# The first expert slot's up products and half of its down products move into attention's instruction list

## The chip, the cores and the metric

The kernel runs on one core of a Trainium2 chip. The metric is the device time of one execution in microseconds (us), compared as the median of several executions. A run's profile is one more execution with the hardware profiler on. PE is the matrix engine, DVE the vector engine, ACT the scalar engine, POOL the general engine, SP the engine whose queue issues most DMAs.

## The reference

Three stages follow each other, all in float32: attention through a packed set of 32 keys, a mixture of 8 experts with one expert per token, and a gated dense layer.

```python
# attention: B=8, H=8, S=576, D=64, 32 packed queries p
p_packed = sm_attn(p, k, v)                 # softmax(p k^T / 8) v
out      = sm_attn(q, p_packed, p_packed)   # softmax(q pp^T / 8) pp
x = out.transpose(0, 2, 1, 3).reshape(4608, 512)
# experts: expert_idx = argmax of cosine(x, expert_emb) / tau
for e in range(8):
    h = np.maximum(x[mask] @ w1[e], 0.0)        # 512 -> 1024
    out[mask] = gate_w[mask, None] * (h @ w2[e])  # 1024 -> 512
# dense: 512 -> 1536 -> 512
return ((x @ w_a) * (x @ w_b)) @ w_out
```

## The kernel before

Attention works through eight batches. For one batch it transposes k (L302), multiplies it with the packed queries (L332, L336), takes the softmax, transposes it (L381) and multiplies it with v (L397): that gives `pp`, the packed values. Then q is transposed (L490), multiplied with `pp` (L528, in two units of 4 and 5 blocks), put through a second softmax on DVE and ACT (L535 to L553), transposed (L560, copied to `aT`), and multiplied with the Gram matrix of `pp` (L581), which gives norms and dot products for the routing (`sq` L590, `nd`).

The experts work in 16 slots of 288 tokens, two for a batch. The kernel takes all tokens of a batch to belong to one expert and falls back to a general path if they don't. Since x = A pp, the first layer is A (pp w1): `zed` computes z = pp w1 (L1008, two products of 16 matmuls a batch), split into a high and a low part (`zh` on ACT, `zl` on DVE). Every expert product is three matmuls of split parts (`mm3`, L816 to L818). A slot has four up products of 24 small steps in two halves, 12 matmuls each, followed by relu (`hh` on ACT, L1069, and `hl` on DVE, L1073), and four down products of 24 matmuls each, followed by a copy to `y` (L1097). w2 is split by `split_w` into `w2h` (ACT, L1039) and `w2l` (DVE, L1040).

Nothing reorders at run time: every engine works through its list in order. The lists are written by a planner (`Sched`), which takes the operations with their engine, cost, priority and buffers, and places at each step the ready operation of the lowest priority number. `SHIFT` adds a number to the priority of each kind of operation; `VB` is a handicap of DVE against ACT for copies that either can do (`evict`). There are two lists: attention's, and then one for the expert slots. `before` puts the first loads, the z products of batch 0 and the splits of its A into attention's list; the slots themselves are in the second list (`static`).

On-chip memory in attention: PSUM holds four one-bank tiles `tr` (transposes, small products) and two two-bank tiles `two` (scores, `pp`, L581, z). The second list has its own PSUM tiles in the same banks, three `up` and two `dn`. Keys and values lie in three tiles each on the right side of SBUF. The w1 loads of a batch and the w2 loads of batch 0 use the same four tiles `raw`, so w2 of batch 0 can be loaded only when both z products of batch 0 are done.

The routing of batches 4 to 7 is the first thing that the second list has in PSUM tile `up` (L743, L744); it goes on to DVE (L747, L748), to POOL for a square root as a power (L751), and back to DVE (L721).

```python
e_ops, g_ops = experts(nc, c, pool(st, "b_rt", side="right", reuse_waits="tile"), KNOWN, B, up0)
e = chain(sch, e_ops, 0.0, c.late, "up", 0.01)
```

Of the kernel before, what the change touches and what calls it, by code (L numbers as in the profile page):

```python
# [7 lines left out]
F32 = mybir.dt.float32  # L8
# [67 lines left out]
class Sched:  # L76
# [96 lines left out]
    "aT_ev.f": -18.7, "aT_mm.f": 98.4, "chain.<lambda>": 59.55, "eT_ev.<lambda>": -79.65,  # L173
    "eT_mm.f": -26.2, "fetch.ar": -2.25, "fetch.pr": -86.75, "kT_ev.<lambda>": 90.1, "kT_mm.f": -142.9,
    "load_k.<lambda>": 20.4, "load_v.<lambda>": 25.1, "make_consts.ev": -33.8, "make_consts.mm": -185.0,
    "ppT_ev.f": 74.65, "pp_mm.f": -143.1, "prep.exp": -130.55, "prep.gr_ev": 11.4, "prep.gr_mm": -194.4,
    "prep.keep": 52.0, "prep.load_p": -79.5, "prep.m8_ev": 0.85, "prep.mx": -10.8, "prep.pT_ev": -78.4,
    "prep.pT_mm": 27.65, "prep.ppT_mm": 43.1, "prep.ppx_a": -211.2, "prep.ppx_ev": -78.55,
    "prep.rs": -114.6, "prep.s1_mm": 226.05, "query.<lambda>": 18.2, "query.qT_ev": 72.75,
    "query.qT_mm": 158.95, "rest.add": 273.9, "rest.dots": -206.3, "rest.exp": 42.6, "rest.mx": 52.8,  # L180
    "rest.norm": -54.4, "rest.s2_mm": -70.25, "rest.sq": 67.35, "rest.sub": 90.45, "rest.total": 172.2,
    "rest.x_mm": -100.75, "split_a.<lambda>": 62.0, "split_w.<lambda>": -222.8, "w1.f": -76.15,
    "w2.f": 35.55, "zed.<lambda>": -92.6, "zed.mm": -87.75}


def attention(ctx, tc, c, q, k, v, p, a_dram, pT_dram, consts, more):
# [28 lines left out]
    S_.LAT, S_.VB, S_.SHIFT, S_.LF = 0.22, 0.25, SHIFT, 4.3  # L215
# [29 lines left out]
    ppT_ops, gr_ops, c.kept, c.a_kept = {}, {}, {}, {}  # L245
# [6 lines left out]
    def prep(b):  # L252
# [58 lines left out]
        for m in (0, 1, 2, 3, 4):  # L311
            t = Buf("tr")
            bkT.append(Buf(f"kT{m}" if m < 4 else "kt"))
            o = op({"T": 0.44}, kT_mm(m), mm=4, deps=[o_k[m // 2]] if m < 4 else o_k, prio=at(0.05 * m), take=[t, bkT[m]],
# [90 lines left out]
        for i0, i1 in ((0, 4), (4, 8), (8, 9)):  # L405
# [4 lines left out]
            mms.append(op({"T": 0.2 * (i1 - i0)}, pp_mm(i0, i1), mm=8 * (i1 - i0), deps=[o] + o_v + mms[-1:], prio=at(0.6 + 0.01 * i0),  # L410
                          take=[] if i0 else [bs], free=[beT] + bv))

        for g in range(2):
# [53 lines left out]
            o = op({"T": 0.42}, gr_mm, mm=10, deps=ppT_ops[b, g], prio=f(0.9), take=[t], free=[bT])  # L467
# [6 lines left out]
    def query(b):  # L474
# [10 lines left out]
        for x in range(5):  # L485
# [14 lines left out]
            o = op({"T": 0.44}, qT_mm, mm=4, deps=o_q + o_qT[-2:-1], prio=pr, take=[tr, bqT[x]], free=bq)  # L500
# [401 lines left out]
class Moe:  # L902


    class Ring:

        def __init__(self, pool, n, shape, dt, name):
            self.t = [pool.tile(shape, dt, tag=f"{name}{i}", name=f"{name}{i}") for i in range(n)]
            self.i = 0
# [8 lines left out]
    def __init__(self, tc, c, pool, raws, a_dram, pT_dram, x2T, w1, w2):  # L918
# [5 lines left out]
        self.ar = [pool.tile([128, 2, S], F32, name=f"ar{i}") for i in range(2)]  # L924
# [5 lines left out]
        self.bufs, self.o_zmm = {}, {}  # L930

    def open(self, pool, up, dn):
        R = self.Ring
        self.r_hh, self.r_hl = R(pool, 4, [128, 2, SLOT], F32R, "hh"), R(pool, 4, [128, 2, SLOT], F32R, "hl")
        self.raw2 = self.raw2[:4] + [pool.tile([128, 1024], F32, name=f"rawb{i}") for i in range(4)]
        self.wt += [[pool.tile([128, 8, 128], F32R, name=f"w2{x}{i}") for x in "hl"] for i in (2, 3)]
        self.r_y = R(pool, 2, [128, 2, SLOT], F32, "y")
        self.r_up = R(up, 3, [128, 2, 512], F32, "up")
        self.r_dn = R(dn, 2, [128, 512], F32, "dn")


    def fetch(self, S, b, p, speak, a_kept, kept):
# [21 lines left out]
        for k in range(4):  # L964
            o = ld[b, "ra", k] = op({"D": 1.46}, w1(k), deps=[speak, first], prio=p + 0.1 * k, take=[Bf(f"ra{k}")],
                                    lat=2.0)
            first = first or o
        ld[b, "pr"] = op({"D": 0.8}, pr, deps=kept, prio=p, take=[Bf("pr")], lat=2.0)
        ld[b, "ar"] = op({"D": 1.6}, ar, deps=[a_kept], prio=p + 0.3, take=[Bf("ar")], lat=2.0)
# [4 lines left out]
    def fetch2(self, S, b, p):  # L974
# [11 lines left out]
        for i in range(4):  # L986
            self.bufs[b, f"rb{i}"] = Buf(f"{n}{i}")
            self.o_ld[b, "rb", i] = op({"D": 1.6}, w2(i), deps=[self.o_ld[b, "ra", 0]], prio=p + 0.1 * i,
                                       take=[self.bufs[b, f"rb{i}"]], lat=2.0)
# [53 lines left out]
    def before(self, S, psum, prio, speak):  # L1043
# [6 lines left out]
        self.zed(S, 0, prio + 1.0, "two", psum)  # L1050
# [3 lines left out]
        for i in range(2):  # L1054
            self.split_w(S, 0, i, prio + 3.0)


# [45 lines left out]
    def static(self, S, speak, flag):  # L1103
# [4 lines left out]
        y_ops = {}  # L1108
# [18 lines left out]
        for s in range(2):  # L1127
            held(None, self.bufs[s, "at"])

# [13 lines left out]
        for s in range(NS):  # L1143
            b, half = divmod(s, 2)
            ups, hls, bh = [], [], []
            for i in range(4):
                bu, st, h = Buf("up"), {}, Buf("h")
                bh.append(h)
                p = s + 0.08 * i

                def mm(e, i=i, st=st, s=s):
                    st["ps"] = self.up_mm(s, i)

                o = op({"T": 1.62}, mm, deps=[self.o_z[b, g, i // 2] for g in range(2)] + [self.o_a[s]], prio=p,
                       take=[bu], free=[self.bufs[s, "at"]] + [self.bufs[b, "z", g, i // 2] for g in range(2)])
                ups.append(o)
# [755 lines left out]
```

## Time and profile before

| what | value |
|---|---|
| median of 3 runs | 1348.51 us (1348.19 to 1353.03) |
| profiled execution, its own time | 1352.98 us |
| its span, first to last instruction | 1350.8 us |
| PE busy / weight loads | 1314.0 us (97%) / 1209.8 us (90%) |
| DVE, ACT, POOL busy | 780.9 (58%), 585.6 (43%), 99.5 us (7%) |
| mean granted clock of PE | 0.993 of full speed |

Busy time of PE counts a matmul from its start to its modelled end, so a busy PE can still be paced by something else; its idle time is certain. The granted clock has two levels here, full (2.4 GHz, shown as 1.0) and half (1.2 GHz); a mean between them says what part of a stretch ran at half.

### The profile page before, as it was taken

Reading aid. Unit: us, or ns where it says so; the run is one execution under the profiler, and the core shown is the slowest. Engines: PE = TensorE matmul, PEld = TensorE weight load, DVE = VectorE, ACT = ScalarE, POOL = GpSimd, SP = SyncE. Lnnn points to the kernel's source line nnn. Section 1 sums busy time; section 2 is a strip of 40 time slices with the busy share of each in tenths; the row PEclk is TensorE's granted clock in tenths of the full one; section 3 lists DMA queues with packets and bytes.
Section 4 is the critical chain, followed back from the end, with each engine's and each line's share of the span. In section 5 each row is a group of like instructions: output and inputs, shape, how many; then the busy total and the mean of one; then the engine's idle time right before and its main releaser. Section 6 shows DMA issues by size and latency. Waiting matters only on the chain.

```text
span 1350.8 us, 25483 instructions
## 1 busy us (share of the span) xinstructions
PE 1314.0 (97%) x9731; PEld 1209.8 (90%) x9731; DVE 780.9 (58%) x1503; ACT 585.6 (43%) x1238; POOL 99.5 (7%) x223
## 2 busy tenths in 40 slices
PE   7999889999999999999999999999999999999997
PEld 6887679999999998999899989999999989999996
DVE  4777866767666828888543454435543563434342
ACT  5765534544444526565432343325332443343232
POOL 1012020010010100000200020002000100001002
PEclk9999989999999999999999999999999999999999
DMA  8875498777797527776855585557656766556552
GB/s 282 285 228 184 155 298 268 249 244 265 227 292 237 181 90 264 240 269 238 251 160 160 158 249 159 160 158 241 170 156 164 228 178 157 162 169 191 162 157 65
DMA packets 169265, 275.34 MB, mean 204 GB/s; under 512 B 18984, under 2 KB 68520, under 8 KB 169136
## 3 DMA queue, kind: packets, MB, share of 16 engines
q1 hardware_dynamic: 162704, 254.72, 61.8%
q0 software_dynamic: 6272, 18.88, 4.0%
q8 instruction: 80, 1.31, 0.4%
q14 instruction: 49, 0.40, 0.1%
q10 hardware_dynamic: 160, 0.02, 0.0%
HBM read 217.99 MB, written 55.57 MB: 203 GB/s over the span
## 4 chain that ended last, share of the span: by engine, by line
PE 91%; DVE 3%; DMA 3%; ACT 1%; issue 1%; POOL 0%; SPq 0%; ACTq 0%; DVEq 0%
PE o L1736 7%; PE o L1737 7%; PE o L1738 7%; PE pb L816 6%; PE pb L818 6%; PE pb L817 6%; PE pa L816 6%; PE pa L818 6%; PE pa L817 6%; PE dn L816 5%; PE dn L818 5%; PE dn L817 5%; PE up L816 3%; PE up L817 2%; PE up L818 2%; DMA out_dram<-osb 2%
## 5 line engine op out<-in xcount | busy, mean ns | idle before, releaser
L1487 DVE TENSOR_TENSOR s<-s,s 128x384 f32<-128x384 f32 x324 | 176.7, 556 | 342.1 <-ACT s L1623 339.6
L816 PE MATMUL pb<-xq,wq 128*128 128x384 f32 x504 | 170.8, 339 | 2.7 <-ACT s L1623 1.1
L816 PE MATMUL pa<-xq,wq 128*128 128x384 f32 x504 | 170.2, 338 | 1.6 <-DVE s L1487 1.6
L1736 PE MATMUL o<-oh,gh 128*128 128x512 f32 x432 | 170.5, 395 | 0.9 <-ACT osb L1756 0.9
L1738 PE MATMUL o<-oh,gl 128*128 128x512 f32 x432 | 170.4, 395 | 0.0
L818 PE MATMUL pa<-xq,wq 128*128 128x384 f32 x504 | 170.3, 338 | 0.0
L1737 PE MATMUL o<-ol,gh 128*128 128x512 f32 x432 | 170.2, 394 | 0.0
L818 PE MATMUL pb<-xq,wq 128*128 128x384 f32 x504 | 170.0, 337 | 0.0
L817 PE MATMUL pb<-xq,wq 128*128 128x384 f32 x504 | 169.8, 337 | 0.0
L817 PE MATMUL pa<-xq,wq 128*128 128x384 f32 x504 | 169.7, 337 | 0.0
L816 PE MATMUL dn<-hh,w2h 128*128 128x288 f32 x512 | 152.6, 298 | 0.0
L1623 ACT COPY s<-pa 128x384 f32<-128x384 f32 x180 | 86.4, 480 | 149.2 <-PE pa L818 149.0
L817 PE MATMUL dn<-hl,w2h 128*128 128x288 f32 x512 | 151.0, 295 | 0.0
L818 PE MATMUL dn<-hh,w2l 128*128 128x288 f32 x512 | 150.6, 294 | 0.0
L1623 ACT COPY s<-pb 128x384 f32<-128x384 f32 x180 | 86.4, 480 | 142.4 <-PE pb L818 142.3
L816 PEld LDWEIGHTS pb<-xq,wq 128*128 128x128 f32 x504 | 94.6, 188 | 13.5 <-DVE c L1487 2.1
L816 PEld LDWEIGHTS dn<-hh,w2h 128*128 128x128 f32 x512 | 95.9, 187 | 9.2 <-ACT hh L1069 3.4
L816 PEld LDWEIGHTS pa<-xq,wq 128*128 128x128 f32 x504 | 94.6, 188 | 9.9 <-DVE s L1487 2.2
L817 PEld LDWEIGHTS pb<-xq,wq 128*128 128x128 f32 x504 | 94.7, 188 | 8.5
L817 PEld LDWEIGHTS pa<-xq,wq 128*128 128x128 f32 x504 | 94.7, 188 | 7.5
L1738 PEld LDWEIGHTS o<-oh,gl 128*128 128x128 f32 x432 | 81.0, 187 | 19.1
L818 PEld LDWEIGHTS dn<-hh,w2l 128*128 128x128 f32 x512 | 96.4, 188 | 0.0
(199 smaller groups left out, 2367.7 us busy)
## 6 DMA issues: line engine op xcount, KB each, us to landing
wq<-ws SPq DMA_DIRECT2D x420, 256.0 KB, 2.8
ws<-wq SPq DMA_DIRECT2D x84, 256.0 KB, 3.8
raw<-in_moe_w_dram SPq DMA_DIRECT2D x36, 512.0 KB, 6.3
rawb<-in_moe_w_dram SPq DMA_DIRECT2D x28, 512.0 KB, 8.2
k<-in_k_dram SPq DMA_DIRECT2D x16, 576.0 KB, 5.1
v<-in_v_dram SPq DMA_DIRECT2D x16, 576.0 KB, 6.3
q<-in_q_dram SPq DMA_DIRECT2D x16, 576.0 KB, 6.3
xr<-x2T SPq DMA_DIRECT2D x20, 384.0 KB, 4.3
```

What stands on the lines that cost most here:

```text
L816: nc.tensor.matmul(ps, lhsT=wh, rhs=xh, start=start, stop=False, **kw)
L817: nc.tensor.matmul(ps, lhsT=wh, rhs=xl, start=False, stop=False, **kw)
L818: nc.tensor.matmul(ps, lhsT=wl, rhs=xh, start=False, stop=stop, **kw)
L1487: VT = lambda out, a, b, o: V.tensor_tensor(out=out, in0=a, in1=b, op=o)
L1623: A.copy(out=T[n, key], in_=ps[n, names_bank[key]])
L1736: nc.tensor.matmul(a, lhsT=gh[:, h, s], rhs=wh, start=first, stop=False)
L1737: nc.tensor.matmul(a, lhsT=gh[:, h, s], rhs=wl, start=False, stop=False)
L1738: nc.tensor.matmul(a, lhsT=gl[:, h, s], rhs=wh, start=False, stop=last)
```

## The change

The four up products and the first two down products of slot 0 are taken out of the second list and put into attention's (`ups` and `downs`, called from `before`). There they use attention's PSUM tiles: up products the two `two` tiles, down products the `tr` tiles. The tiles for relu's results (`hh`, `hl`) and for `y` are opened in the middle of attention's list: the pool that holds keys and values moves to the left side of SBUF, is closed by `swap`, and the new pool takes its place once the last transposes of k and the last products with v are placed. One of the two tiles for A, `ar1`, moves from a pool that lives from the start to one that is opened with the second list. The number of matmuls, their shapes and what they compute stay as they are.

With it go new planner numbers: all of `SHIFT`, `VB` from 0.25 to 0.45, a cost of four kinds of PE work, and a delay of 4.0 instead of 2.0 for the first expert's loads. So attention's whole order is another one. For instance the first loads were p, k, k, v and are now k, k, k, p. Over the whole program 16 small copies go from DVE to ACT (40 such copies were on DVE, 24 are).

```diff
-    "aT_ev.f": -18.7, "aT_mm.f": 98.4, "chain.<lambda>": 59.55, "eT_ev.<lambda>": -79.65,
+    "aT_ev.f": 118.2, "aT_mm.f": -41.15, "before.<lambda>": -65.3, "chain.<lambda>": 161.7,
...
-    for name, pools in dict(io="kvq", kt=["pT", "pz", "kt"] + [f"kT{m}" for m in range(4)], q=["qT"], e=["e", "eT"],
+    for name, pools in dict(io="q", kt=["pT", "pz", "kt"] + [f"kT{m}" for m in range(4)], q=["qT"], e=["e", "eT"],
...
+    sb.update(k=c.kv, v=c.kv)
...
-    S_.LAT, S_.VB, S_.SHIFT, S_.LF = 0.22, 0.25, SHIFT, 4.3
+    S_.LAT, S_.VB, S_.SHIFT, S_.LF = 0.22, 0.45, SHIFT, 4.3
...
         for i in range(2):
             self.split_w(S, 0, i, prio + 3.0)
-
+        self.r_up, self.r_dn = two, one
+        room = S.op({"none": 0.0}, lambda e: self.open_h(c.swap()), deps=c.over(), prio=prio)
+        self.hls, self.bh = self.ups(S, 0, prio + 4.0, "two", [room])
+        self.downs(S, 0, prio + 5.0, "tr", self.hls, self.bh, range(2))
...
+            hls, bh = self.ups(S, s, s, "up") if s else (self.hls, self.bh)
+            if s % 2 == 0:
+                ahead(s // 2 + 1)
+            self.downs(S, s, s + 0.34, "dn", hls, bh, range(4) if s else (2, 3))
...
+        def swap():
+            kv.close()
+            return pool(left, "b_h", reuse_waits="tile")
...
+                c.over = lambda: list(c.last.values())
```

How the lists change at three places. First ACT around the first relu results. Before, these rows stand at the end of attention's list and the start of the second:

```order
L1014 CAST zh<-two 128x2x512
L234 COPY aT<-tr 128x2x192
L234 COPY aT<-tr 128x2x128
L1014 CAST zh<-two 128x2x512
L1039 CAST w2h_107<-raw_94 128x1024
L1039 CAST w2h_109<-raw_95 128x1024
L1069 ACTIVATE hh_3096<-up_3114 128x576
L1039 CAST w2h_3108<-raw_96 128x1024
L1069 ACTIVATE hh_3097<-up_3115 128x576
```

Now, with both z products and their `zh` already earlier in the list, ACT has there (L1119 is the relu, L1049 the split of w2):

```order
L1119 ACTIVATE hh_2787<-two 128x576
L237 COPY aT<-tr 128x2x192
L1049 CAST w2h_106<-raw_94 128x1024
L237 COPY qT<-tr 128x512
L547 ACTIVATE as_206<-as_206 128x16x32
L1119 ACTIVATE hh_2788<-two 128x576
L1049 CAST w2h_108<-raw_95 128x1024
L1119 ACTIVATE hh_2789<-two 128x576
```

The first relu no longer stands behind splits of w2, the second stands behind one; between them is work of attention's last batch.

Second PE, in the changed kernel, where the first up product stands between attention's products (L447 belongs to `pp` of the last batch, L820 to L822 are `mm3`, L564 transposes the second softmax, L532 is q times `pp`; of the 12 matmuls of the product the last six are shown):

```order
L820 MATMUL two<-ath_102,zh 128x288
L821 MATMUL two<-atl_103,zh 128x288
L822 MATMUL two<-ath_102,zl 128x288
L820 MATMUL two<-ath_102,zh 128x288
L821 MATMUL two<-atl_103,zh 128x288
L822 MATMUL two<-ath_102,zl 128x288
L564 MATMUL tr<-ident,an 128x128 x3
L532 MATMUL two<-ppT_209,qT 64x2x32
```

In the order of PE there follow: more of attention, up products 2 and 3, transposes of q, up product 4, the second unit of the last batch's scores, 16 rows of L585 (the Gram product), down product 1, 36 rows of L585, five transposes, down product 2, the last 20 rows of L585. Then the second list begins, with two up products of slot 1, the routing product, the other two down products of slot 0, and the third up product of slot 1. Before, all of slot 0 stood behind the last L581.

Third DVE at the start of the second list. Before (L1073 is `hl`, L747, L748 and L721 are the routing of batches 4 to 7, L1030 the split of A):

```order
L747 COPY ndt_3125<-up_3114 128x288
L748 TENSOR_SCALAR r_3128<-up_3114 128x36
L1073 SCALAR_TENSOR_TENSOR hl_3102<-up_3116,hh_3098 128x576
L1073 SCALAR_TENSOR_TENSOR hl_3103<-up_3115,hh_3099 128x576
L1030 TENSOR_TENSOR atl_104<-ar_99,ath_103 128x576
L721 TENSOR_SCALAR r_3128<-r_3128,tau 128x36
L721 RECIPROCAL r_3128<-r_3128 128x36
```

Now (L1123 is `hl`, here of slot 1; L751, L752 and L725 are the routing, L1040 the split of A, L1050 of w2):

```order
L1050 TENSOR_TENSOR w2l_3231<-raw_96,w2h_3230 128x1024
L1050 TENSOR_TENSOR w2l_3233<-raw_97,w2h_3232 128x1024
L1040 TENSOR_TENSOR atl_103<-ar_3225,ath_102 128x576
L751 COPY ndt_3245<-up_3236 128x288
L752 TENSOR_SCALAR r_3248<-up_3236 128x36
L725 TENSOR_SCALAR r_3248<-r_3248,tau 128x36
L725 RECIPROCAL r_3248<-r_3248 128x36
L1123 SCALAR_TENSOR_TENSOR hl_2791<-up_3234,hh_2787 128x576
```

The `hl` of the tile `up_3234` now stands behind the routing's two steps that need POOL's result, and these behind the split of A of batch 1. The third up product of slot 1 writes the same tile `up_3234`.

## Rows read from the trace of the kernel before

**Rows 1.** Busy time by stretch: PE, PEld, DVE, ACT, POOL; then clock, DMA share, GB/s.

```profile
20.00:150.00 130.00, 125.57 (x2490) 103.90 (x2482) 100.84 (x248) 82.98 (x227) 16.86 (x11) 0.99 0.69 223
150.00:205.00 55.00, 45.33 (x515) 39.29 (x515) 39.02 (x72) 20.95 (x38) 9.44 (x5) 0.91 0.76 251
205.00:400.00 195.00, 195.00 (x1530) 186.44 (x1530) 134.23 (x211) 87.38 (x142) 17.55 (x24) 1.00 0.81 261
400.00:1330.00 930.00, 924.00 (x5060) 861.16 (x5058) 495.77 (x938) 378.96 (x802) 44.66 (x135) 1.00 0.63 187
```

**Rows 2.** Timeline of PE, 150 to 200 us: start, length, idle before and its releaser.

```profile
157.15 0.59 PE L581 MATMUL two<-gr,aT 64*64 64x72 f32 x19 [0.68 <-issue]
...
162.53 0.77 PE L560 MATMUL tr<-ident,an 128*128 128x128 f32 x5 [1.79 <-DVE an L553]
...
176.20 1.64 PE L743 MATMUL up<-nd,pair 128*128 128x288 f32 x4 [4.26 <-DVE hl L1073]
...
197.31 0.58 PE L816 MATMUL up<-ath,zh 128*128 128x288 f32 x1 [1.82 <-DVE hl L1073]
```

**Rows 3.** Timeline of ACT, 171 to 175 us.

```profile
171.40 1.05 ACT L1039 CAST w2h<-raw 128x1024 fp32r<-128x1024 f32 x1 [4.51 <-DMA raw<-in_moe_w_dram]
...
174.12 0.64 ACT L1069 ACTIVATE hh<-up 128x576 fp32r<-128x576 f32 x1
```

**Rows 4.** Timeline of PE within one down product: every third matmul is L816.

```profile
182.31 0.29 PE L816 MATMUL dn<-hh,w2h 128*128 128x288 f32 x1
...
188.31 0.30 PE L816 MATMUL dn<-hh,w2h 128*128 128x288 f32 x1
```

**Rows 5.** Chain that ended last, 0 to 260 us: start, length, what.

```profile
120.41 0.79 PE two L581 x40
...
124.88 0.97 PE tr L743 x4
...
163.75 1.96 PE two L1008 x16
165.72 1.24 PE two L581 x40
...
203.89 1.02 PE up L1008 x16
```

**Rows 6.** The same chain, finer, 165 to 204 us.

```profile
180.05 0.24 PE up L817
...
195.52 0.39 ACT y L1097
195.91 0.56 ACT hh L1069
196.49 0.77 DVE hl L1073
```

**Rows 7.** Timeline of DVE, 178 to 187 us.

```profile
178.99 0.45 DVE L747 COPY ndt<-up 128x288 f32<-128x288 f32 x1
179.36 0.19 DVE L748 TENSOR_SCALAR r<-up 128x36 f32<-128x36 f32 x1
...
185.84 0.24 DVE L721 TENSOR_SCALAR r<-r,tau 128x36 f32<-128x36 f32 x1 [2.81 <-POOL r L751]
186.12 0.38 DVE L721 RECIPROCAL r<-r 128x36 f32<-128x36 f32 x1
```

**Rows 8.** Line L751 on POOL: ns of one, least, median, most.

```profile
L751 POOL TENSOR_TENSOR r<-r,half x2: 6117/6130/6143, 128.7 to 179.7; 128x36 f32<-128x36 f32 x2
```

**Rows 9.** DMA issues, 165 to 200 us: count, KB each, median us to landing.

```profile
rawb<-in_moe_w_dram SPq DMA_DIRECT2D x4, 512.0 KB, 8.7
...
ar<-a_dram SPq DMA_DIRECT2D x2, 576.0 KB, 6.1
```

**Rows 10.** Timeline of PE, at the start and at 84 us.

```profile
8.08 4.53 PE L302 MATMUL tr<-ident,k 128*128 128x128 f32 x20 [1.17 <-DMA k<-in_k_dram]
...
83.87 0.56 PE L528 MATMUL two<-ppT,qT 128*64 128x64 f32 x10 [1.61 <-issue]
```

More of the change, by code (lines that the diff above doesn't have):

```diff
@@ L313, in prep @@
             bkT.append(Buf(f"kT{m}" if m < 4 else "kt"))
-            o = op({"T": 0.44}, kT_mm(m), mm=4, deps=[o_k[m // 2]] if m < 4 else o_k, prio=at(0.05 * m), take=[t, bkT[m]],
+            o = c.last[b, m] = op({"T": 0.48}, kT_mm(m), mm=4, deps=[o_k[m // 2]] if m < 4 else o_k, prio=at(0.05 * m), take=[t, bkT[m]],
                    free=[bk[m // 2]] if m < 4 else bk)
@@ L409, in prep @@
             o = op(evict(128 * (i1 - i0)), eT_ev(i0, i1), deps=[o], prio=at(0.45 + 0.01 * i0), free=[t])
-            mms.append(op({"T": 0.2 * (i1 - i0)}, pp_mm(i0, i1), mm=8 * (i1 - i0), deps=[o] + o_v + mms[-1:], prio=at(0.6 + 0.01 * i0),
-                          take=[] if i0 else [bs], free=[beT] + bv))
+            c.last[b, "v"] = op({"T": 0.26 * (i1 - i0)}, pp_mm(i0, i1), mm=8 * (i1 - i0), deps=[o] + o_v + mms[-1:], prio=at(0.6 + 0.01 * i0),
+                          take=[] if i0 else [bs], free=[beT] + bv)
+            mms.append(c.last[b, "v"])
         for g in range(2):
@@ L905, with __init__ @@
     class Ring:
-        def __init__(self, pool, n, shape, dt, name):
-            self.t = [pool.tile(shape, dt, tag=f"{name}{i}", name=f"{name}{i}") for i in range(n)]
-            self.i = 0
+        def __init__(self, tiles):
+            self.t, self.i = tiles, 0
         def __call__(self):
@@ L1041, in split_w, with before @@
             out=lo, in0=src, in1=hi.bitcast(F32), op=ALU.subtract), deps=[o], prio=p, free=[self.bufs[b, f"rb{i}"]])
-    def before(self, S, psum, prio, speak):
+    def before(self, S, two, one, prio, speak):
         c = self.c
@@ L1055, in before, with ups, up, downs @@
             self.split_w(S, 0, i, prio + 3.0)
+        self.r_up, self.r_dn = two, one
+        room = S.op({"none": 0.0}, lambda e: self.open_h(c.swap()), deps=c.over(), prio=prio)
+        self.hls, self.bh = self.ups(S, 0, prio + 4.0, "two", [room])
+        self.downs(S, 0, prio + 5.0, "tr", self.hls, self.bh, range(2))
+    def ups(self, S, s, p, bank, extra=()):
+        b, hls, bh = s // 2, [], []
+        for i in range(4):
+            bu, st, h = S.Buf(bank), {}, S.Buf("h")
+            bh.append(h)
+            def up(e, i=i, st=st):
+                st["ps"] = self.up_mm(s, i)
+            o = S.op({"T": 1.62}, up, deps=[self.o_z[b, g, i // 2] for g in range(2)] + [self.o_a[s]] + list(extra),
+                     prio=p, take=[bu], free=[self.bufs[s, "at"]] + [self.bufs[b, "z", g, i // 2] for g in range(2)])
+            o = S.op({"A": 0.65}, lambda e, i=i, st=st: self.relu(i, st["ps"]), deps=[o], prio=p, take=[h])
+            hls.append(S.op({"V": 0.75}, lambda e, i=i, st=st: self.relu_lo(i, st["ps"]), deps=[o], prio=p, free=[bu]))
+            p += 0.08
+        return hls, bh
+    def downs(self, S, s, p, bank, hls, bh, tiles):
+        b, by = s // 2, None
+        for i in tiles:
+            bd, st = S.Buf(bank), {}
+            q = p + 0.16 * i
+            if i % 2 == 0:
+                by = S.Buf("y")
+            def down(e, i=i, st=st):
+                st["ps"] = self.down_mm(i)
+            o = S.op({"T": 3.22}, down, deps=hls[:3] + [self.o_w[b, i]], prio=q, take=[bd],
+                     free=[self.bufs[b, "w", i]] + bh, after=hls[3])
+            o = S.op({"A": 0.4}, lambda e, s=s, i=i, st=st: self.out(s, i, st["ps"]), prio=q,
+                     deps=[o], take=[] if i % 2 else [by], free=[bd])
+            self.y_ops[s, i] = o
+            if i % 2:
+                S.op({"none": 0.0}, lambda e: None, deps=[o], free=[by], prio=q, lat=0.0)
     def up_mm(self, s, fp):
@@ L1107, in static @@
         NONE = {"none": 0.0}
-        y_ops = {}
+        y_ops = self.y_ops
         def held(o, b, free=()):
@@ L1128, in static @@
             held(None, self.bufs[s, "at"])
+        for b in self.bh:
+            held(None, b)
         for k in (2, 3):
```

93 lines of the change are left out of this document (36 added, 57 removed).

## Prediction

> **What bounds the kernel now.** I read the busy times by stretch first. From 205 us to 1330 us PE is busy for 1119 of 1125 us at full clock, and from 20 to 150 us for 125.6 of 130 [rows 1]. A change that leaves the number of matmuls alone can win only where PE stands or runs at half clock. That is mostly one place: from 150 to 205 us PE is busy for 45.3 of 55 us at a mean clock of 0.91 [rows 1]. Then I read PE's timeline there. The reader is to see four waits: one for issue, one for DVE's `an` in the tail of attention, then 4.26 us for the first `hl`, and 1.82 us for another [rows 2].
>
> The long one is explained on ACT. The second list has ACT split w2 before the first relu. Those splits wait for their load, since w2 goes into the tiles that the z products have just finished reading; ACT stands 4.51 us for it, and the first relu comes at 174.12 us [rows 3], after `up` products that PE had finished more than two microseconds earlier. PE has three `up` tiles, all full, and stands. The wait of 1.82 us is the chain `y` 0.39, `hh` 0.56, `hl` 0.77 after a last down product [rows 6]: the relu tiles are free only when the down products that read them are done.
>
> What is lost from 150 to 205 us is thus 55 - 45.3 = 9.7 us of standing [rows 1], and the half clock. Of that the mean allows at most 0.09 x 55 = 5.0 us. By pieces: a z product took 1.96 where the same takes 1.02, 40 Gram matmuls 1.24 where 0.79 is usual, the routing product 1.64 for 0.97 [rows 5]. An expert matmul takes 0.24 [rows 6] where it takes 6.00 / 45 = 0.133 at full clock [rows 4], and 23 of them ran so (9 after the routing product, 14 after the wait of 1.82), which makes 2.5. Together 0.94 + 0.45 + 0.67 + 2.5 = 4.6 us. The sum is 14.3 us.
>
> **The change, part by part.** Matmuls: 48 of up and 48 of down products move, none is added: 96 x 0.133 = 12.8 us of PE work that now lies between attention's last products instead of behind them. It costs nothing by itself and it is the cover for DVE's chain there.
>
> The switch (4.26 us). The first relu now stands on ACT before the first split of w2, and later relus behind one split each. Both z products stand together and early, so the w2 loads are issued earlier against what needs them. From the z products' end to the second up product PE has the first up product (12 x 0.133 = 1.6 us), one unit of q times `pp`, the small products of the last `pp` and some seventeen transposes, by my estimate from those rows 5 to 6 us. Before, ACT took the first w2 tile at 171.40 us [rows 3], 5.7 us after the second z product, which began at 163.75 and took 1.96 [rows 5], had freed it. I take this wait as gone. If its cover fails, each microsecond that the load is late costs one.
>
> The tail (0.68, 1.79 and three smaller ones, together 3.5 of the 9.7). They wait for DVE or issue while nothing else is in PE's list. Now the expert products are. Against it stands the ring of two `two` tiles: an up product holds one for its matmuls 1.6, a relu of 0.64 [rows 3] and an `hl` of 0.77 [rows 6], about 3 us, and scores and Gram products of the last batch need the same two. Ten such takings at 3 us on two tiles are 15 us, and PE has some 25 us of work there, so it should be covered. On DVE four `hl` and two `w2l` come in, some 5.5 us, and PE's own list grows by 12.8. I leave 1.0 us of handing over; the bounds are 0 and the old 3.5.
>
> The wait of 1.82 us stays and grows. Slot 1's first two up products fill two `up` tiles, the routing product the third, and the third up product needs the first one back, whose relu waits for slot 0's last down product: again `y`, `hh`, `hl`. But on DVE that `hl` is now behind the routing's step that waits for POOL. POOL's power takes 6.13 us [rows 8], and DVE stood 2.81 us for it before, when nothing behind it was wanted at once [rows 7]. Counted from the end of the routing product: `ndt` 0.45, `r` 0.19, power 6.13, two steps 0.24 and 0.38 [rows 7, 8], `hl` 0.77, some 0.3 between engines, 8.5 us; PE has two down products meanwhile, 48 x 0.133 = 6.4. So it would stand 2.1 us. `ndt` in turn is behind `atl`, which needs A of batch 1. That load is issued behind attention's last store: from the last copy of `aT`, four issues of about 0.4, 6.1 to landing [rows 9], and splits of 0.67 and 0.75, together 9.1 us, after two copies of 0.75 in all. PE from the last transposes to the end of the routing product has 24 + 24 expert matmuls (6.4), 40 Gram matmuls (0.79) and the routing (0.97 and a little): 8.3. So `ndt` is 1.4 to 1.6 us late and the wait is about 3.5 us. Bounds: 1.8 if the chain hides, 6.1 if A lands like the slowest loads there, 8.7 after issue [rows 9]. PE has then stood, and after 1.82 us it ran 14 matmuls at half clock: 1.5 us, bounds 0 and 1.5.
>
> The Trainium skill, DMA: Bandwidth & Descriptors, section Anatomy of one DMA, gives a DMA a fixed 2.0 us and its bytes at 436 GB/s. By it A (576 KB) would land 3.4 us after its issue, the routing would not be late, the wait would be 2.1 us and the time 1338.9 us. The trace disagrees with 6.1 us [rows 9], and the sum keeps the trace.
>
> The start. The k loads are issued first and p after three of them. PE's first transposes waited for k until 8.08 us [rows 10]; they may start a microsecond earlier, but p is now transposed after k, and its copy stands before the first scores. I take 0, bounds 1.2 either way.
>
> The 16 copies that go from DVE to ACT, the new order of the eight batches and the moved pools: between 20 and 150 us PE stands 4.4 us in all [rows 1], the longest 1.61 us for issue [rows 10]. A new order may lose that or add its like; I take 0. The loads of k, v and q wait for the same readers as before. The cover of all these is PE's own dense list; without it a copy costs its own length, and 16 moved ones are then a gain on DVE and a loss on ACT.
>
> Sum: of 14.3 us there stay 3.5 + 1.5 + 1.0 = 6.0, gain 8.3 us. The profiled execution took 1352.98 us with a span of 1350.8, so it would become 1344.7. That execution is 4.5 us above the median of the runs, at the upper of them (1353.03). Whether the 4.5 us lie in the stretch that I count can't be read from one profile; I apply the whole gain to the median: 1348.5 - 8.3 = **1340.2 us**.
>
> **Rivals.**
> First, a clean handover: the routing's chain hides behind the down products, only 1.8 us stay, and no half clock follows. Gain 12.5, 1336.0 us. For it: PE's work up to there may be longer than I count. Against it: the DVE order shown.
>
> Second, the tail doesn't flow: a relu behind a late w2 split keeps one `two` tile, and the other goes round alone. Then the old 3.5 us of the tail come back, with another stretch at half clock of 1.5 us: 10.0 us stay, gain 4.3, 1344.2 us. For it: ACT has two splits and softmax steps between the relus, and the load of w2 is behind stores of `pp` on SP. Against it: ACT was busy for 21.0 of 55 us there [rows 1].
>
> Third, slower: attention's own new order, at the dense runs of small matmuls between 20 and 150 us. The old order has one place where PE stands 1.61 us for issue [rows 10] and then runs at half clock, which by the stretch's mean of 0.99 [rows 1] costs at most 1.3 us more: 2.9 us. Three such places more eat the gain; six give 17.4 - 8.3 = 9.1 us slower, 1357.6 us. For it: every kind of work in attention got a new priority, so runs of small matmuls meet at other places than before. Against it: the costs of four kinds of PE work were raised, which spreads them.
>
> The Trainium skill, Runtime: NRT & Kernel Launch, section Instruction fetch mechanics, holds that fetching instructions is mostly hidden. If the waits for issue are that, they should be rare and this rival weaker; the trace shows a few, up to 1.61 us.
>
> **How the numbers follow.** My forecast 0.45, the clean handover 0.20, the tail 0.20, attention's order 0.15, of which 0.08 with five places or more and 0.07 with fewer. A measurement of this kernel can tell about 0.5% (6.7 us) from no change. The forecast and the clean handover are faster by more: 0.65. The tail and the milder form of the third are within it: 0.27. Slower: 0.08. The low end takes the clean bounds (1.8 us of waits, a start 1.2 us earlier, 1334.8) and the loss of the old issue wait of 2.9: 1332. The high end takes 6.1 + 1.5 + 3.5 and a later start: 1346.5. What is left out is the third rival and a little. The forecast alone lies from 1337 to 1343.
>
> **What would show it.** In the changed profile: no wait of 4 us for `hl` at the switch, PE busy through attention's last 20 us with up products among small ones; a wait of 2 to 5 us before slot 1's third up product, ended by `hl`, with DVE waiting for POOL just before, and PE at half clock after it; about the same standing between 20 and 150 us. From there on the old course, some 8 us earlier. I am wrong if PE stands for `hh`, `hl` or w2 in the tail, if the wait at the third up product is gone, or if attention up to its last batch is longer by more than a few microseconds.

## The result and the profile after

The change takes 1335.27 us (median of 6 runs, 1334.51 to 1337.35), against 1351.05 us for the kernel before on the same chip (6 runs, 1348.19 to 1354.36). The ratio is 0.9885 (95% interval 0.9864 to 0.9905): 1.15% or 15.5 us faster, where 8.3 us were forecast. The profiled executions, 1352.98 and 1336.29 us, have spans of 1350.8 and 1334.2 us, 16.6 us apart.

The busy times by stretch answer to [rows 1], with the same columns:

```profile
20.00:150.00 130.00, 129.36 (x2569) 107.74 (x2562) 108.38 (x251) 94.12 (x254) 15.98 (x10) 1.00 0.77 252
150.00:205.00 55.00, 51.17 (x542) 47.73 (x541) 39.63 (x69) 22.48 (x41) 9.24 (x5) 0.97 0.71 239
205.00:400.00 195.00, 194.69 (x1539) 185.79 (x1538) 131.26 (x207) 86.70 (x141) 18.22 (x25) 1.00 0.80 260
400.00:1330.00 930.00, 917.95 (x4943) 853.78 (x4941) 491.18 (x937) 376.17 (x799) 48.57 (x153) 1.00 0.62 185
```

From 150 to 205 us PE now stands 3.8 us where it stood 9.7. But it also stands 0.6 us where it stood 4.4 between 20 and 150 us, which the forecast took as unchanged. The table of PE's waits up to 205 us (total, times, longest) answers to [rows 2, 10]; `enps` is a transpose of the expert embeddings that now stands first in PE's list:

```profile
PE enps L67 <- POOL as L215: 6.6, 1, 6.6
PE up L820 <- DVE hl L1123: 3.8, 1, 3.8
PE tr L384 <- ACT e L356: 1.3, 1, 1.3
PE two L335 <- ACT pT L237: 0.6, 1, 0.6
PE tr L564 <- POOL an L557: 0.5, 1, 0.5
```

The wait of 4.26 us at the switch, the waits in the tail and every wait for issue are gone. One is left and has grown from 1.82 to 3.83 us. The chain that ended last shows how it comes about (start, length, what; short pieces left out):

```profile
162.49 0.83 PE two L585 x40
163.33 5.14 DMA ar<-a_dram
168.49 0.68 ACT ath L1039
169.20 0.76 DVE atl L1040
169.96 0.37 DVE ndt L751
...
170.58 6.14 POOL r L755
176.75 0.26 DVE r L725
...
177.32 0.71 DVE hl L1123
178.07 0.61 PE up L820
178.68 0.24 PE up L821
```

The load of A (`ar`) lands 5.14 us after its start; its split on DVE holds back the routing's `ndt`, POOL's power takes 6.14 us, and only then comes the `hl` that frees the tile which slot 1's third up product writes. Behind it PE runs at half clock, 0.24 us a matmul where 0.133 is usual [rows 4, 6].

To divide the 16.6 us, three marks: the last product of `pp`, the first dense product, the end. PE's timeline of before (start, length, what), then of after:

```profile
144.42 1.32 PE L397 MATMUL two<-v,eT 64*64 64x128 f32 x40
...
502.29 0.34 PE L816 MATMUL pa<-xq,wq 128*128 128x384 f32 x1
```

```profile
135.11 1.49 PE L400 MATMUL two<-v,eT 64*64 64x128 f32 x48
...
483.23 0.34 PE L820 MATMUL pa<-xq,wq 128*128 128x384 f32 x1
...
1064.35 0.50 PE L1757 MATMUL o<-oh,gh 128*128 128x512 f32 x1 [2.06 <-ACT osb L1777]
```

The last matmul of the first `pp` product starts at 21.18 us instead of 23.21, of the last at 136.33 instead of 145.48, and the first dense product at 483.23 instead of 502.29. So the start gives 2.0 us, attention between its first and last `pp` product 7.1 us (122.27 to 115.15), and the stretch from there to the dense stage 9.9 us (356.8 to 346.9). The dense stage gives 2.5 us back: from its first product to the end 848.5 us before and 851.0 after, with the wait of 2.06 us shown last. That part varies between executions. In the profiles of the experiments it is 846.8 to 851.3 us, so the first dense product is a better mark than the profile's end. A mark still belongs to one execution, and the medians decide.

In the profile of before PE also runs at half clock from 84.7 to 88.1 us, right behind its wait of 1.61 us for issue. The busy times of 75 to 100 us show it as a mean clock of 0.93 (columns as in [rows 1]); after has no half clock there:

```profile
75.00:100.00 25.00, 23.34 (x481) 19.66 (x474) 17.91 (x41) 15.36 (x43) 2.31 (x2) 0.93 0.67 216
```

### The profile page after: what moved, and what is told of

It is laid out like the page before. It is cut to its first block, busy times and chain, and to the rows that moved or that the text cites. A ratio compares the mean times of both kernels' runs of the same rounds, so it can differ in the third digit from the quotient of the medians.

```text
span 1334.2 us, 25519 instructions
## 1 busy us (share of the span) xinstructions
PE 1304.6 (98%) x9731; PEld 1205.1 (90%) x9731; DVE 777.6 (58%) x1489; ACT 589.5 (44%) x1254; POOL 97.0 (7%) x221
## 4 chain that ended last, share of the span: by engine, by line
PE 88%; DMA 4%; DVE 3%; ACT 2%; POOL 1%; issue 1%; SPq 0%; ACTq 0%; DVEq 0%; POOLq 0%
PE o L1757 7%; PE o L1758 7%; PE o L1759 7%; PE pb L820 6%; PE pb L822 6%; PE pb L821 6%; PE pa L820 6%; PE pa L822 6%; PE pa L821 6%; PE dn L820 4%; PE dn L821 4%; PE dn L822 4%; DMA out_dram<-osb 2%; PE up L820 2%; PE up L822 2%; PE up L821 2%
## 5 line engine op out<-in xcount | busy, mean ns | idle before, releaser
L820 PE MATMUL pb<-xq,wq 128*128 128x384 f32 x504 | 171.0, 339 | 2.2 <-DVE s L1508 0.7
L820 PE MATMUL pa<-xq,wq 128*128 128x384 f32 x504 | 170.5, 338 | 1.6 <-DVE s L1508 1.6
L822 PE MATMUL pa<-xq,wq 128*128 128x384 f32 x504 | 170.6, 339 | 0.0
L822 PE MATMUL pb<-xq,wq 128*128 128x384 f32 x504 | 170.0, 337 | 0.0
L821 PE MATMUL dn<-hl,w2h 128*128 128x288 f32 x496 | 146.8, 296 | 1.1 <-DVE hl L1123 1.1
L820 PE MATMUL dn<-hh,w2h 128*128 128x288 f32 x496 | 147.7, 298 | 0.0
L822 PE MATMUL dn<-hh,w2l 128*128 128x288 f32 x496 | 147.1, 296 | 0.0
L820 PEld LDWEIGHTS pb<-xq,wq 128*128 128x128 f32 x504 | 94.8, 188 | 13.1 <-DVE c L1508 2.2
L820 PEld LDWEIGHTS pa<-xq,wq 128*128 128x128 f32 x504 | 94.8, 188 | 10.0 <-DVE s L1508 2.3
L821 PEld LDWEIGHTS pa<-xq,wq 128*128 128x128 f32 x504 | 94.8, 188 | 7.5
L820 PEld LDWEIGHTS dn<-hh,w2h 128*128 128x128 f32 x496 | 93.7, 189 | 7.5 <-ACT y L1147 2.5
L822 PEld LDWEIGHTS pa<-xq,wq 128*128 128x128 f32 x504 | 94.9, 188 | 0.0
```

What stands on the lines that cost most here:

```text
L820: nc.tensor.matmul(ps, lhsT=wh, rhs=xh, start=start, stop=False, **kw)
L821: nc.tensor.matmul(ps, lhsT=wh, rhs=xl, start=False, stop=False, **kw)
L822: nc.tensor.matmul(ps, lhsT=wl, rhs=xh, start=False, stop=stop, **kw)
```

## The experiments

Each was timed beside the kernel before on its chip; "ratio" is against that one, with its 95% interval. "First to last `pp`" and "first dense product" are read from its profile as above.

| kernel | median us | ratio | first to last `pp` | first dense product |
|---|---|---|---|---|
| before | 1348.99 to 1351.05 | 1 | 122.3 | 502.3 |
| the change | 1335.27 | 0.9885 (0.9864 to 0.9905) | 115.2 | 483.2 |
| numbers alone | 1341.84 | 0.9947 (0.9929 to 0.9965) | 115.0 | 490.5 |
| move alone | 1348.18 | 0.9980 (0.9964 to 0.9997) | 119.4 | 497.4 |
| routing late | 1336.80 | 0.9909 (0.9891 to 0.9927) | 115.0 | 484.0 |
| A told later | 1334.64 | 0.9895 (0.9877 to 0.9914) | 115.0 | 482.8 |
| before, 64 tiny matmuls | 1351.33 | 1.0027 (1.0013 to 1.0041) | 117.8 | 495.8 |
| the change, 64 tiny | 1334.45 | 0.9901 (0.9884 to 0.9918) | 115.0 | 483.6 |
| `hl` first | 1330.11 | 0.9860 (0.9839 to 0.9881) | 115.1 | 480.2 |
| costs alone | 1358.27 | 1.0077 (1.0054 to 1.0099) | 121.5 | 505.3 |
| before, 32 tiny | 1347.86 | 0.9980 (0.9966 to 0.9994) | 117.0 | 500.1 |
| the change, 32 tiny | 1338.73 | 0.9919 (0.9904 to 0.9934) | 118.6 | 489.8 |
| `hl` first, six tiles | 1328.78 | 0.9851 (0.9834 to 0.9867) | 115.0 | 476.7 |
| six tiles alone | 1329.22 | 0.9845 (0.9828 to 0.9863) | 115.7 | 478.9 |

**Numbers alone.** The new planner numbers, with all of slot 0 back in the second list:

```diff
...
-        self.hls, self.bh = self.ups(S, 0, prio + 4.0, "two", [room])
-        self.downs(S, 0, prio + 5.0, "tr", self.hls, self.bh, range(2))
...
-            hls, bh = self.ups(S, s, s, "up") if s else (self.hls, self.bh)
+            hls, bh = self.ups(S, s, s, "up")
...
-            self.downs(S, s, s + 0.34, "dn", hls, bh, range(4) if s else (2, 3))
+            self.downs(S, s, s + 0.34, "dn", hls, bh, range(4))
```

> Left as before: all of slot 0 is in the second list again. Kept: the new planner numbers, the pools and so attention's new order up to its last batch. My theory: attention's order alone is worth 9 to 10 us (end of the last pp product near 137 us from the span's start, not 145.5), and the switch keeps its long wait for the first hl of about 4 us, the tail its small waits. So 9 us faster than before, about 1342 us, 6 to 7 us slower than the change. Rival A, the one of the prediction (attention's order is worth nothing): 1349 to 1352 us, as before. Rival B, the move is worth nothing and the numbers are all: 1335 to 1337 us, as the change.

The time came out as my theory had it, 8 us faster than before, and attention up to its last `pp` product is as in the change. But the waits are others than I expected; PE's from 137 to 205 us:

```profile
PE tr L564 <- DVE an L557: 4.9, 1, 4.9
PE up L820 <- DVE hl L1120: 1.8, 1, 1.8
PE two L585 <- DVE aT L239: 0.8, 1, 0.8
PE two L585 <- ACT aT L237: 0.7, 1, 0.7
...
```

There is no wait of 4 us for the first `hl`: the new order has both z products at 137 us, and w2, which is loaded behind them, is there in time without the move. PE's timeline shows the two z products, ACT's the first split of w2, which waits for no load:

```profile
137.16 1.95 PE L1018 MATMUL two<-raw,pr 64*32 64x512 f32 x32
```

```profile
143.36 1.05 ACT L1049 CAST w2h<-raw 128x1024 fp32r<-128x1024 f32 x1
```

Instead the last softmax chain on DVE lies open. PE stands 4.92 us for `an` and then runs at half clock. In the change, slot 0's products lie over that chain.

**Move alone.** The new lists and pools, with all planner numbers of before (`SHIFT`, `VB`, costs, delays):

```diff
...
-    S_.LAT, S_.VB, S_.SHIFT, S_.LF = 0.22, 0.45, SHIFT, 4.3
+    S_.LAT, S_.VB, S_.SHIFT, S_.LF = 0.22, 0.25, SHIFT, 4.3
...
```

> Kept: slot 0's first products and half of its second ones are in attention's list. Left as before: all planner numbers, so attention's PE order is the one of before, and the planner puts the moved products behind attention's last Gram product, where they stood before; only the first relu on ACT now stands behind one w2 split and not two. My theory: the move without the numbers brings the switch wait down by one split at most, 0 to 3 us faster than before, 1347 to 1351 us, with the last pp product ending near 145.5 us. Rival (the move by itself is what gains, by the early relu): the 4.26 us wait is gone and 8 us or more are won, 1343 us or less.

As expected, almost nothing: 0.2% faster. The planner with the old numbers puts slot 0 behind attention's last Gram product again. The wait for `hl` falls from 4.26 to 2.47 us, where the first relu on ACT has one split fewer ahead of it, but a wait of 1.19 us for `sq` comes in ahead of the up products, so that the switch still costs 3.7 us. PE's waits:

```profile
...
PE two L818 <- DVE hl L1121: 2.5, 1, 2.5
PE tr L562 <- DVE an L555: 2.4, 2, 1.8
...
PE two L530 <- issue: 1.9, 1, 1.9
PE two L818 <- DVE sq L592: 1.2, 1, 1.2
...
```

By the ratios the numbers are worth 0.53% alone, the move 0.20%, both together 1.15%: the rest, 0.4% or 6 us, is the interleaving that needs both.

**Routing late.** The routing of batches 4 to 7 gets later priorities in the second list:

```diff
-            e = chain(sch, e_ops, 0.0, c.late, "up", 0.01)
+            e = chain(sch, e_ops, 1.2, c.late, "up", 0.01)
```

(Its followers get 1.8 and 2.0 for 0.6 and 1.0.)

> The change with one thing altered: the routing of batches 4 to 7 comes later in the second list, so that on PE slot 1's third up product does not wait for hl behind POOL's power. My theory (the 3.8 us wait and the half clock behind it are the POOL chain and the late A of batch 1): the wait falls to 2 us or less, half clock may stay, 2 to 4 us faster than the change, 1331.5 to 1333.5 us. Rival (the wait is set by slot 0's down products and their relu tiles alone, the POOL chain only runs beside it): wait 3 to 4 us as in the change, 1335 us.

The wait fell as the theory said, to 1.83 us with no half clock behind it, and nothing was won. The routing's steps on DVE now stand in front of slot 2's `hl`, PE waits 2.81 us there and runs at half clock from 203.6 to 207.0 us:

```profile
176.59 1.24 PE L747 MATMUL up<-nd,pair 128*128 128x288 f32 x4 [1.83 <-DVE hl L1123]
...
202.68 0.40 PE L820 MATMUL up<-ath,zh 128*128 128x288 f32 x1 [2.81 <-DVE hl L1123]
```

So neither theory was whole: the wait does follow POOL's chain, but the chain's work on DVE only moved in front of another `hl`.

**A told later.**

```diff
-        ld[b, "ar"] = op({"D": 1.6}, ar, deps=[a_kept], prio=p + 0.3, take=[Bf("ar")], lat=2.0 if b else 4.0)
+        ld[b, "ar"] = op({"D": 1.6}, ar, deps=[a_kept], prio=p + 0.3, take=[Bf("ar")], lat=4.0 if b == 0 else 5.5 if b == 1 else 2.0)
```

> The change with one thing altered: the planner is told that A of batch 1 lands later (a delay of 5.5 instead of 2.0), so on DVE the routing's two first steps stand ahead of the split of A of batch 1 and POOL's power starts earlier. My theory (1.4 to 1.6 us of the wait of 3.8 are A's late landing, ahead of the routing on DVE): wait about 2.2 us, 1 to 2 us faster than the change, 1333.5 to 1334.5 us. Rival (A's landing sets hl anyway, since its split stays ahead of hl): the wait stays at 3.5 to 4 us, 1335 us.

POOL starts 2.0 us earlier than in the change (170.58 there), but the wait only falls by 0.64 us, since the planner uses the time for two more routing steps ahead of `hl`. The wait is thus between those of theory and rival, and the time is not told apart from that of the change. POOL's and PE's timelines:

```profile
168.58 6.13 POOL L755 TENSOR_TENSOR r<-r,half 128x36 f32<-128x36 f32 x1 [4.36 <-DVE r L752]
```

```profile
177.49 0.40 PE L820 MATMUL up<-ath,zh 128*128 128x288 f32 x1 [3.19 <-DVE hl L1123]
```

**Tiny matmuls in front.** What are attention's waits for issue? In the DMA view, queue 8 of kind "instruction" moves packets of 16 KB, 80 of them in the execution of the change (packets, MB, share of 16 engines' span):

```profile
q8 instruction: 80, 1.31, 0.4%
```

Against 2 x 9731 matmuls and weight loads that makes 243 for each, so I take it for the queue of PE's instructions and call such a packet a fetch. In the kernel before one such packet starts at 81.55 us, and PE stands until 83.87 us [rows 10]. The others start at 50.14, 103.25 and 116.60 us, and the waits end at 52.53, 105.59 and 118.84: 2.24 to 2.39 us later each. To test it, the same orders were put behind a number of tiny matmuls that run while PE has nothing to do:

```diff
+    pad = c.ps_tr.tile([128, 512], F32, tag="tr", name="tr")
+    for _ in range(64):
+        nc.tensor.matmul(pad[0:8, 0:8], lhsT=c.ident[0:8, 0:8], rhs=c.ident[0:8, 0:8], start=True, stop=True)
     return S_.run()
```

> The kernel before with 64 tiny matmuls (8x8, with their weight loads some 128 instructions of PE) put in front of everything, while PE waits for p; every later row of PE stands 128 instructions further back, the orders are the same. My theory: PE's issue waits come where a 16 KB instruction fetch of PE's queue falls into a dense run of small matmuls (in the kernel before each ends 2.2 to 2.4 us after such a fetch starts), so the five places at 52, 62, 82, 105 and 118 us change: some waits go, others may come, and their sum between 20 and 150 us (5.0 us at four places named in the profile and two shorter ones) changes by more than 1 us. Rival (they belong to the order of the matmuls alone): issue waits at the same five rows, 1.6 us or more for the q times pp product of the 83 us place, sum as before.

> The change with the same 64 tiny matmuls in front of everything. Theory (where a fetch falls is luck): the change has no issue wait only because its fetches fall well; moved on by 128 instructions, one or more issue waits of 0.3 us or more appear before 165 us and it loses 0.5 to 3 us, 1336 to 1338 us. Rival (the new order spreads the dense runs, so that a fetch is never late): none appears, 1335 us as the change. The tiny matmuls themselves lie beside the wait for enps, 6.6 us, and cost nothing.

I had the size wrong. One such matmul leaves two records of PE and two of weight loads: 256 more records on both, about one fetch, and the kernel before has 81 such packets with them in place of 80. So rows and fetches were moved by about the same amount, and this pair tests little. (Also, the four waits of the profile of before add up to 3.27 us, not to the 5.0 I had written.) The longest wait of the kernel before stayed at its place (after 21 matmuls of its product instead of 22), the others up to 150 us went, and the change got none, as the rival had it, at 1334.45 us. The profile of before with 64 has attention 4.5 us shorter, but by the medians this kernel is 0.27% slower; that is not explained, and the profiled execution was the fastest of its 12. PE's timeline of before with 64:

```profile
81.61 0.56 PE L528 MATMUL two<-ppT,qT 128*64 128x64 f32 x11 [1.33 <-issue]
```

With 32 of them, half a fetch:

> The kernel before with 32 tiny matmuls in front in place of 64. The run with 64 showed 257 more records on PE and its weight loads, about one fetch of 16 KB: the fetches fell at the same rows again, and the long issue wait in the product of the 83 us place came at the same row. With 32 the rows move by half a fetch. Theory (an issue wait comes where a fetch starts late in a dense run): the wait of 1.6 to 2.1 us in that product at its 21st row is gone or at another row by dozens, and the sum of issue waits between 20 and 150 us differs from 3 to 5 us by more than 1 us. Rival (the order alone): a wait of 1.5 us or more at the 20th to 22nd row of that product again.

> The change with 32 tiny matmuls in front: its rows stand half a fetch further back. With a whole fetch (64 of them) no issue wait came, as nothing moved against the fetches. Theory (the change has none by the luck of its fetches): one or more of 0.3 us or longer before 165 us, 1336 to 1338 us. Rival (the new order leaves every fetch time): none, 1334 to 1336 us.

In the profiles both came out as the theory had it. In the kernel before all waits for issue between 20 and 150 us are gone, and PE is busy for 128.40 us there in place of 125.57 [rows 1]; by the medians that is worth 0.20%, 2.8 us:

```profile
20.00:150.00 130.00, 128.40 (x2578) 106.01 (x2570) 104.22 (x255) 85.36 (x234) 18.50 (x12) 0.99 0.72 235
```

In the change, which had none, four appear, and it loses 3.5 us by the medians, a little more than I expected:

```profile
52.97 0.67 PE L400 MATMUL two<-v,eT 64*64 64x128 f32 x16 [0.29 <-issue]
...
58.89 0.41 PE L335 MATMUL two<-kT,pT 64*32 64x256 f32 x3 [0.33 <-issue]
...
78.64 0.82 PE L494 MATMUL tr<-ident,q 128*128 128x128 f32 x6 [0.82 <-issue]
...
139.56 0.45 PE L400 MATMUL two<-v,eT 64*64 64x128 f32 x7 [0.44 <-issue]
```

The packet ahead of the third is in the DMA view of 76.3 to 76.4 us (packets, MB, share); PE goes on 2.33 us after its start at 76.31:

```profile
q8 instruction: 1, 0.02, 61.1%
```

The same order without padding doesn't always have the same waits. Move alone has attention's old order and, up to its last `pp` product, two waits for issue (1.91 and 0.63 us) where the profile of before has four (3.27 us); it needs 2.9 us less there. The new order has none in six profiles without padding and one in the seventh, that of six tiles alone, told below; its table of waits has:

```profile
PE two L532 <- issue: 0.4, 1, 0.4
```

So the place in the list is not all that decides.

**Costs alone.** The kernel before with the raised costs and `VB` 0.45, old `SHIFT`, no move:

```diff
...
-            o = op({"T": 0.42}, gr_mm, mm=10, deps=ppT_ops[b, g], prio=f(0.9), take=[t], free=[bT])
+            o = op({"T": 0.59}, gr_mm, mm=10, deps=ppT_ops[b, g], prio=f(0.9), take=[t], free=[bT])
...
```

(The costs of k, q and `pp` become 0.48, 0.48 and 0.26.)

> The kernel before with only the raised costs of four kinds of PE work and DVE's higher handicap for copies; SHIFT, slots, pools and loads as before. It is another order of attention. Theory (the raised costs spread the dense runs, which is what removes the issue waits): the issue waits between 20 and 150 us fall from 5 us to 1 us or less, 3 to 5 us faster than before. Rival (each order is a new draw of where fetches fall): issue waits of 1 to 5 us at other places, within 3 us of before either way.

Both were wrong on the time: 0.8% slower. Issue waits did fall to 1.0 us (0.74 and 0.24), but PE now waits for other engines all through attention. It stands 8.4 us from 20 to 150 us (busy 121.62). So the raised costs alone are not what makes the new order good. PE's waits up to 215 us, the longest ones and the longer of the two for issue:

```profile
...
PE tr L560 <- DVE an L553: 3.5, 1, 3.5
PE two L528 <- ACT qT L234: 2.4, 1, 2.4
PE tr L560 <- POOL an L553: 2.2, 1, 2.2
...
PE two L336 <- issue: 0.7, 1, 0.7
...
```

**`hl` first.** To the edit of "A told later" come a longer told time for POOL's power in the second list and a later priority for the steps behind it:

```diff
-        ("P", 0.5 + 0.15 * n, root, "")] + V(d), [
+        ("P", 0.5 + (0.22 if b0 else 0.15) * n, root, "")] + V(d), [
...
-            e = chain(sch, e_ops, 0.0, c.late, "up", 0.01)
+            e = chain(sch, e_ops[:3], 0.0, c.late, "up", 0.01)
+            e = chain(sch, e_ops[3:], 1.1, [e], "up", 0.01)
```

> The change with the order on DVE altered at the start of the second list, by telling the planner a longer time for POOL's power there and a later landing of A of batch 1, and by putting the steps behind the power at a later priority: the routing's first two steps stand ahead of the split of A, the first two hl of slot 1 ahead of the steps that need POOL. PE's order stays as in the change up to the z products. My theory (the wait of 3.8 us is 1.8 us for y, hh, hl after the last down product, and 2.0 us that the routing and A's landing add): the wait falls to 1.8 to 2.2 us with nothing lost behind, 1.5 to 3 us faster than the change, 1332 to 1333.5 us. Rival (the work of DVE that is put off stands in front of a later hl, as in the run with the routing late): 1335 to 1337 us with a wait of 2 us or more between 190 and 210 us.

The wait is 1.83 us, the chain of `y`, `hh`, `hl` alone, and no other comes up to 205 us. The first dense product is 3.0 us earlier than in the change; by the medians 5 us are gained, more than I expected, with intervals of the ratios that overlap a little:

```profile
176.47 0.43 PE L820 MATMUL up<-ath,zh 128*128 128x288 f32 x1 [1.83 <-DVE hl L1123]
```

**Six tiles.** Then the root of those 1.8 us, the relu tiles, with the edit of "`hl` first" and without it:

```diff
-    SIZES = dict(up=3, dn=2, h=4, y=2, at=2, ar=2, pr=1,
+    SIZES = dict(up=3, dn=2, h=6, y=2, at=2, ar=2, pr=1,
...
-        self.r_hh, self.r_hl = R(pool, 4, shape, "hh", F32R), R(pool, 4, shape, "hl", F32R)
+        self.r_hh, self.r_hl = R(pool, 6, shape, "hh", F32R), R(pool, 6, shape, "hl", F32R)
```

> The run with hl first (1330 us), and six tiles each for hh and hl in place of four. My theory (the 1.8 us that are left there are relu tiles waiting for slot 0's last down product, and the half clock behind comes from PE's standing): with two more tiles slot 1's first relus need not wait, the wait and the half clock from 177 to 180 us go, 2 to 3.5 us faster, 1327 to 1328 us. Rival (something else on DVE or ACT sets it, A's split or the y copies): a wait of 1 us or more remains before slot 1's third up product, 1329 to 1331 us.

> The change with one thing altered: six tiles each for hh and hl in place of four; costs, priorities and the routing's place as in the change. The planner then sets the first two hl of slot 1 ahead of the routing on DVE, since their tiles are free. My theory (the wait of 3.8 us has one root, the relu tiles; the POOL chain and A's late landing lengthen it only because hl comes out behind them): wait and half clock from 178 to 181 us both go, 4 to 5.5 us faster than the change, 1330 to 1331.5 us, about as the run with hl first and six tiles together. Rival (the POOL chain holds PE by itself): a wait of 2 us or more before slot 1's third or fourth up product, 1333 us or more.

With both, PE stands 0.50 us between 150 and 205 us, there is no half clock between the start and the last 5 us, and the time is 1328.78 us:

```profile
150.00:205.00 55.00, 54.50 (x580) 51.51 (x579) 41.27 (x71) 24.25 (x44) 9.74 (x5) 1.00 0.86 283
```

Six tiles alone do nearly all of it: 1329.22 us, and in place of the 3.8 us wait two short ones:

```profile
PE up L1018 <- DVE hl L1123: 0.9, 1, 0.9
...
PE dn L821 <- DVE hl L1123: 0.5, 1, 0.5
```

With six tiles the planner also sets slot 1's first two `hl` ahead of the routing on DVE, so this run has another order there as well:

```profile
168.28 1.41 DVE L1123 SCALAR_TENSOR_TENSOR hl<-up,hh 128x576 fp32r<-128x576 f32 x2
```

The order alone (`hl` first) leaves 1.83 us, the tiles with the order that follows from them 0.9 and 0.5. So I take the four relu tiles for the root of the wait: POOL's chain and the late A lengthen it because a relu that waits for its tile comes out behind them. Six tiles with the old order on DVE were not tried. Both kernels beat the change: their runs took 1327.65 to 1330.31 us, those of the change 1334.51 to 1337.35 us.

## Why the prediction was right, and where not

- **The switch wait gone.** Right: no wait of that kind is left. Its cause was only half named. The two early z products remove it without an early relu (numbers alone). The early relu without early z products only shortens it, from 4.26 to 2.47 us, with 1.19 us for `sq` ahead of it (move alone).
- **The tail, 3.5 to 1.0 us.** Right, and better than forecast: from 150 us to the second list PE has no wait. That this is the work of the interleaved products is shown by numbers alone, where PE without them stands 4.92 us for `an`.
- **The wait at slot 1's third up product, 3.5 us, and half clock of 1.5 behind it.** Right in place and in the chain, 3.83 us measured; that the relu tiles are what lets POOL's chain in front is what "Six tiles" adds. A landed after 5.14 us instead of the 6.1 of [rows 9], and `ndt` was still late. By the Trainium skill's price (3.4 us, DMA: Bandwidth & Descriptors, Anatomy of one DMA) A would not have been late; the trace keeps disagreeing with that. The section fits its price to DMAs that the general engine issues, and this load is on SP's queue, so the prediction used it too widely; its own sum with that price is 1338.8 us, not 1338.9. Half clock: 0.24 us for each matmul up to 181.2 us.
- **Sum of this stretch.** Of 14.3 us there stay 3.8 of standing (55 - 51.17) and by my estimate 1.5 of half clock (the mean clock of 0.97 allows 0.03 x 55 = 1.65), 5.3 in place of 6.0: a gain of 9.0 where 8.3 was forecast.
- **Attention's new order, forecast 0.** This is the step that failed: 7.1 us between the first and the last `pp` product, and not about the same standing there. In these two profiles 3.8 us of it are standing (4.43 and 0.64 us between the two products), of which waits for issue make 3.27. About 1.7 us more are the half clock from 84.7 to 88.1 us, for which the third rival allowed 1.3. Half a fetch of padding takes both from the old order (122.3 to 117.0) and gives the new one waits (115.2 to 118.6), so I take these losses to depend on where fetches fall; but two executions of the old order without padding differ by 2.9 us too (122.3 and 119.4), so a part of the 7.1 belongs to the one execution that was profiled. The two orders, both without issue waits, differ by 1.9 us, although the new one has done 40 more Gram matmuls and 5 more transposes by the last `pp` product; this part is the order itself. Rival three had the mechanism, issue waits that come or go with the order, and only the losing sign. The loss of the old waits stood only in the low end of the range, as 2.9 us, and had no chance of its own.
- **The start, forecast 0 within 1.2.** Off by more: 2.0 us earlier. PE now waits 6.6 us once for `enps` and not for p and k; and the half clock from 16.5 to 19.9 us of the profile of before did not come. It was not tested by itself, but the old order behind 64 tiny matmuls has no half clock there either, and its first `pp` product is 1.4 us earlier (21.82 us).
- **Behind the switch, old course.** Nearly: the profiled execution gives 2.5 us back in the dense stage, which differs as much between executions of other kernels here.

By the marks the profiled executions give 2.0 + 7.1 + 9.9 - 2.5 = 16.5 of 16.6 us. Of the 9.9 the stretch above explains 9.0. The 45 matmuls and transposes that the new order has done earlier would add some 1.6 (40 Gram matmuls take 0.79 us in [rows 5], five transposes 0.77 us in [rows 2]), and PE's further standing from 205 us to the dense stage, 2.3 us in place of 0.8, takes about as much away; 0.9 us is left open.

That the time lies in the range is in part luck. Its low end was made of a clean handover, which did not come, and of an earlier start and the loss of one old issue wait, which both came larger than there. The time is also nearly the 1336.0 us of the first rival, whose mechanism (POOL's chain hidden, no half clock) did not happen. By the ratios half a fetch of padding is worth 0.20% to the old order and costs the new one 0.34%, almost a third of the change's gain, and with the unlucky position (1338.73 us) the change would have come out near the forecast.

## What to carry to other kernels

A gain of moved work is only there if the list's order interleaves it: here the move alone gave 0.2%, the numbers alone 0.5%, both 1.15%. When a new order is to be judged, list the old one's waits for issue as a possible gain as well as a possible loss, and try a few paddings of the instruction stream before believing a difference of 0.3%. Where a wait is a long chain through several engines, look for the buffer at its root: two more tiles for each of `hh` and `hl`, with the order that the planner then writes, did what reordering the chain did only in part.

## What the hardware showed beyond that

Packets of 16 KB come on a DMA queue of kind "instruction", one for about 243 matmuls and weight loads of PE, and I read the waits for issue as PE running dry while one is on its way. Fourteen waits for issue between 20 and 150 us, in six of the fourteen profiles here (0.24 to 1.91 us), ended 2.2 to 2.6 us after such a packet's start, each amid small matmuls or transposes. The Trainium skill (Runtime: NRT & Kernel Launch, Instruction fetch mechanics) has the blocks of 16 KB and holds that crossing one is mostly hidden. Here the blocks agree, most crossings show nothing (the fourteen profiles have some 290 packets in that stretch), and the ones that show cost up to 1.91 us each. What makes one fetch late and the next not is not shown.
